# Seven block products in place of eight in the channel half of an MLP-mixer, with the token products of all batches ahead of it

## The chip, the core and the metric

The kernel runs on one core of one Trainium2 chip. The metric is device time in microseconds (us): the median of three runs was 979.88 us (979.80 to 980.96). Five engines work side by side, each on its own queue in order: TensorE (PE, with its weight loads shown as PEld), VectorE (DVE), ScalarE (ACT), GpSimd (POOL) and SyncE (SP, which issues the transfers). Semaphores order them. TensorE writes to PSUM; VectorE and ScalarE take results out of it.

## What is computed

A clustered attention, and behind it one mixer layer. Sizes: 4 batches, 8 heads of 64, sequence 768, model width 512, token width 256, channel width 1536. All is float32 (the weights arrive as float64).

```python
attn_out = _attn_ref(**attn_kwargs)          # masked softmax attention, (B, H, S, D)
x = attn_out.transpose(0, 2, 1, 3).reshape(B, S, H * D)
xt = x.transpose(0, 2, 1)
h = np.maximum(xt @ w_tok1, 0.0) @ w_tok2    # token products
u = x + h.transpose(0, 2, 1)
h2 = np.maximum(u @ w_ch1, 0.0) @ w_ch2      # channel products
return (u + h2)
```

## The kernel before

**Attention** fills the first 373 us: 16 pairs of heads, six steps each, written as one loop over `m` in which scores, exponentials, sums and values of neighbouring steps alternate. While it runs, the float64 weights of the token products and of the first channel product are turned into float32 pieces: ScalarE makes two parts (L184, L186), VectorE three operations (L191, L196, L201), GpSimd one addition (L208). The attention result of batch b lies in `xs[b]`, six blocks of 128 tokens by 512.

**Token products** of a batch: `tok1` (L439), two groups of six 128x512 matmuls with a relu behind each (L427 on VectorE, L429 on ScalarE in turn), then `tok2` (L448), six groups of two, each followed by an addition into `xs[b]` on VectorE (L451). Those of batch 0 come right behind the attention, those of batch b+1 among the channel products of batch b.

**Channel products** go by half batches of 384 tokens: `turn_u` transposes u on TensorE (L460, twelve 128x128) and ScalarE copies it out (L463); `ch1` (L470) makes twelve groups of four 128x384 matmuls, relu behind each; `ch2` (L479) three groups of twelve 128x512 matmuls, an addition on VectorE (L484) and a transfer out (L485). A float32 matmul stands in the profile as two MATMUL records, called passes here, each with a weight load of its own.

**Order.** Nothing reorders the work: each engine's queue holds the instructions in the order in which the program's lines make them (the lists `ends` and `weights` say what is made beside what). The weights of `ch2` are converted during the first `ch1` groups. Behind batch 0, `fits` (L493 to L507) checks with a few VectorE operations and one tiny matmul (L504) that the fast path was valid, and every engine loads three counts into a register (L512), which decides at the program's end whether the general path runs.

Of the kernel before, what the change touches and what calls it, by code (L numbers as in the profile page):

```python
# [18 lines left out]
P = 128  # L19
NJ = S // P  # L20
# [26 lines left out]
def kernel(  # L47
# [46 lines left out]
    h1pool = pool("h1pool", 1)  # L94
# [15 lines left out]
    ohs = [const.tile([P, 2, NJ, P], BF16, name=f"oh{i}") for i in range(2)]  # L110
# [3 lines left out]
    wt1 = const.tile([P, NJ, DTOK], F32, name="wt1")  # L114
    wt2 = const.tile([P, NT, NJ, P], F32, name="wt2")
    wc1 = const.tile([P, NF, DCH], F32, name="wc1")
# [25 lines left out]
    def weight_pieces(names):  # L142

        if "tok" in names:
            src = moe_w_tok1.rearrange("(p j) t -> p (j t)", p=P)
            dst = wt1.rearrange("p j t -> p (j t)")
            for c in range(0, NJ * DTOK, WMAX):
                yield dst[:, c : c + WMAX], src[:, c : c + WMAX]
            for t in range(NT):
                for p0 in range(0, P, P // 2):  # L150
                    yield (
                        wt2[:, t, :, p0 : p0 + P // 2].rearrange("t j p -> t p j"),
                        moe_w_tok2[t * P : (t + 1) * P, p0 * NJ : (p0 + P // 2) * NJ],
                    )
        if "ch1" in names:
            for c in range(0, DCH, WMAX):
                for f in range(NF):
                    yield wc1[:, f, c : c + WMAX], moe_w_ch1[f * P : (f + 1) * P, c : c + WMAX]
        if "ch2" in names:
            for ct in range(NCT):  # L160
                yield pools["wc2"][:, ct], moe_w_ch2[ct * P : (ct + 1) * P]

    def weight_steps(pool, names):
# [46 lines left out]
        pieces = list(weight_pieces(names))  # L210
# [211 lines left out]
    turns = [0]  # L422
# [13 lines left out]
    def tok1(b, t):  # L436
        pf = mtile([P, DM], "ph1")
        for j in range(NJ):
            nc.tensor.matmul(  # L439
                pf, lhsT=wt1[:, j, t * P : (t + 1) * P], rhs=xs[b][:, j],  # L440
                start=(j == 0), stop=(j == NJ - 1),
            )
        relu(h1[:, t], pf)

    def tok2(b, j):
        pu = mtile([P, DM], "pu")
        for t in range(NT):
            nc.tensor.matmul(  # L448
                pu, lhsT=wt2[:, t, j], rhs=h1[:, t], start=(t == 0), stop=(t == NT - 1)
            )  # L450
        nc.vector.tensor_tensor(out=xs[b][:, j], in0=pu, in1=xs[b][:, j], op=ALU.add)  # L451

    uTs = {}

    def turn_u(b, hf):
        uT = uTs[b, hf] = pools["mlp"].tile([P, NF, HJ, P], F32, name="uT", bufs=2)
# [19 lines left out]
    def ch2(b, hf, i):
        po = mtile([P, DM], "po2")
        for ct in range(NCT):
            nc.tensor.matmul(  # L479
                po, lhsT=pools["h2"][:, ct, i * P : (i + 1) * P], rhs=pools["wc2"][:, ct],  # L480
# [102 lines left out]
    for item in ends:  # L583
        item()
# [235 lines left out]
```

## Time and profile before

| | us |
|---|---|
| median of three runs | 979.88 |
| the profiled execution's own time | 979.91 |
| its span (first to last instruction) | 978.1 |
| PE busy | 953.1 (97%) |
| DVE busy | 364.5 (37%) |
| ACT busy | 263.2 (27%) |
| POOL busy | 48.8 (5%) |

Durations of instructions are from the one profiled execution. A busy time is the union of an engine's instructions; matmuls overlap each other, so the mean of one pass is longer than the distance from pass to pass. In the chain of waits the row "PE pc L470 x96" with 30.96 us means 96 passes one behind the other.

### The profile page before, as it was taken

To read this page: it belongs to the slowest core of one execution; us is meant where nothing else is said; L and a number is where in the kernel's file an instruction comes from. 1 tells how busy PE (TensorE), PEld (TensorE's weight loads), DVE (VectorE), ACT (ScalarE), POOL (GpSimd) and SP (SyncE) were. 2 spreads that over 40 slices of the span, in tenths; PEclk is the share of its full clock that TensorE was granted. 3 is DMA by queue.
4 is the path that set the end of the run, shared out by engine and by line. 5 is a ranking of instruction groups with operands and counts; after the bars stand their busy time and mean duration, and the time that the engine had idled before them with its cause. 6 is when DMAs were issued, how large, how long until landed. Compare 5 with 4: busy or idle time off the path is not lost.

```text
span 978.1 us, 10328 instructions
## 1 busy us (share of the span) xinstructions
PE 953.1 (97%) x4227; PEld 461.8 (47%) x4227; DVE 364.5 (37%) x554; ACT 263.2 (27%) x421; POOL 48.8 (5%) x40
## 2 busy tenths in 40 slices
PE   4999999999999999999999899999999999999997
PEld 2444444444444444554544454554554554554553
DVE  4778777787878652660102100101100101100100
ACT  3655566566565552430000010000110000110000
POOL 1001101010111000230000000000000000000000
PEclk9999999999999999999999999999999999999999
DMA  9253433333342001320000000000000000000000
GB/s 194 66 102 78 86 92 71 92 70 93 72 111 46 1 23 43 108 87 25 8 0 22 11 1 21 11 0 11 21 1 21 11 1 11 22 0 22 11 8 29
DMA packets 112823, 41.68 MB, mean 43 GB/s; under 512 B 101632, under 2 KB 105728, under 8 KB 112768
## 3 DMA queue, kind: packets, MB, share of 16 engines
q1 hardware_dynamic: 109632, 40.55, 16.8%
q10 hardware_dynamic: 3136, 0.39, 0.3%
q8 instruction: 35, 0.57, 0.3%
q14 instruction: 20, 0.16, 0.1%
HBM read 34.64 MB, written 6.29 MB: 42 GB/s over the span
## 4 chain that ended last, share of the span: by engine, by line
PE 97%; DVE 1%; ACT 1%; DMA 0%; issue 0%; ACTq 0%; DVEq 0%; SPq 0%
PE po L479 25%; PE pc L470 25%; PE sc L340 17%; PE av L369 14%; PE pu L448 4%; PE ph L439 4%; PE px L404 2%; PE po L316 1%; PE pr L278 1%; PE den L385 1%; PE pt L460 1%; DMA raw<-in_moe_w_ch_dram 0%; ACTq L133 0%; DVE qkT L267 0%; DVE x L484 0%
## 5 line engine op out<-in xcount | busy, mean ns | idle before, releaser
L470 PE MATMUL pc<-uT,wc 128*128 128x384 f32 x768 | 251.4, 489 | 1.6 <-issue 1.6
L479 PE MATMUL po<-wc,h 128*128 128x512 f32 x576 | 249.5, 592 | 0.0
L470 PEld LDWEIGHTS pc<-uT,wc 128*128 128x128 f32 x768 | 146.3, 191 | 104.0 <-issue 6.1
L346 ACT ACTIVATE ex<-sc 128x768 f32<-128x768 f32 x192 | 145.3, 808 | 117.3 <-PE sc L340 117.3
L479 PEld LDWEIGHTS po<-wc,h 128*128 128x128 f32 x576 | 109.2, 190 | 135.3 <-issue 133.7
L369 PE MATMUL av<-ex,va 128*64 128x384 f32 x768 | 145.1, 499 | 0.0
L359 DVE TENSOR_TENSOR sum<-sum,ex 128x768 f32<-128x768 f32 x128 | 133.5, 1043 | 30.6 <-ACT ex L346 22.2
L340 PE MATMUL sc<-qkT 64*128 64x384 f32 x768 | 140.7, 486 | 0.0
L429 ACT ACTIVATE h<-pc 128x384 f32<-128x384 f32 x48 | 23.6, 492 | 359.2 <-PE pc L470 359.2
L484 DVE TENSOR_TENSOR x<-po,x 128x512 f32<-128x512 f32 x24 | 16.6, 691 | 261.5 <-PE po L479 261.5
L427 DVE TENSOR_SCALAR h<-pc 128x384 f32<-128x384 f32 x48 | 26.8, 557 | 189.2 <-PE pc L470 189.2
L369 PEld LDWEIGHTS av<-ex,va 128*64 128x64 f32 x768 | 46.6, 136 | 86.5 <-issue 82.7
L340 PEld LDWEIGHTS sc<-qkT 64*128 64x128 f32 x768 | 71.2, 188 | 31.8 <-issue 0.6
L340 PE MATMUL sc<-ohT 64*128 64x384 bf16 x384 | 48.5, 329 | 1.8 <-ACT ohT L318 1.0
L208 POOL TENSOR_TENSOR wc<-wT,wup 128x512 int32<-128x512 int32 x24 | 35.5, 1480 | 259.8 <-DVE wT L201 143.3
L448 PE MATMUL pu<-h,wt 128*128 128x512 f32 x96 | 42.1, 593 | 0.0
L463 ACT COPY uT<-pt 128x384 f32<-128x384 f32 x32 | 13.0, 491 | 107.9 <-PE pt L460 107.9
L439 PE MATMUL ph<-x,wt 128*128 128x512 f32 x96 | 42.0, 593 | 0.0
L410 DVE TENSOR_TENSOR x<-px,rcps 128x384 f32<-128x384 f32 x32 | 17.8, 557 | 49.5 <-PE px L404 47.9
L355 DVE TENSOR_TENSOR sum<-ex 128x768 f32<-128x768 f32 x32 | 30.2, 944 | 6.3 <-ACT ex L346 5.7
L267 DVE STREAM_TRANSPOSE qkT<-qk 128x768 f32<-128x768 f32 x32 | 29.3, 953 | 0.0
L439 PEld LDWEIGHTS ph<-x,wt 128*128 128x128 f32 x96 | 18.2, 190 | 22.4 <-issue 21.6
(63 smaller groups left out, 376.1 us busy)
## 6 DMA issues: line engine op xcount, KB each, us to landing
raw<-in_moe_w_ch_dram SPq DMA_DIRECT2D x24, 512.0 KB, 3.8
qk<-in_k_dram SPq DMA_DIRECT2D x64, 96.0 KB, 4.0
va<-in_v_dram SPq DMA_DIRECT2D x16, 384.0 KB, 3.4
out_dram<-x SPq DMA_DIRECT2D x24, 256.0 KB, 2.0
qk<-in_q_dram SPq DMA_DIRECT2D x60, 96.0 KB, 3.0
raw<-in_moe_w_tok_dram SPq DMA_DIRECT2D x3, 512.0 KB, 5.3
raw<-in_moe_w_tok_dram SPq DMA_DIRECT2D x4, 384.0 KB, 3.6
qk<-in_q_dram ACTq DMA_DIRECT2D x4, 96.0 KB, 3.5
```

Source lines behind the costliest of these rows:

```text
L208: nc.gpsimd.tensor_tensor(out=dst.bitcast(I32), in0=T, in1=up, op=ALU.add)
L267: nc.vector.transpose(out=st["T"][:, a].rearrange("p j t -> p (j t)"), in_=st["qk"][:, a].rearrange("p j i d -> p (j i d)"),)
L340: nc.tensor.matmul(scs[i][:, h, 0:HS], lhsT=src[rows, 1, j0 + i], rhs=src[rows, 0, js], start=start, stop=not start,)
L346: nc.scalar.activation(out=ex, in_=scs[i][:, :, 0:HS], func=ACT.Exp, scale=SM_SCALE)
L355: nc.vector.tensor_tensor(out=acc, in0=e[0], in1=e[1], op=ALU.add)
L359: nc.vector.tensor_tensor(out=acc, in0=acc, in1=e[i], op=ALU.add)
L369: nc.tensor.matmul(st["av"][h * D : (h + 1) * D], lhsT=st["va"][:, h, j], rhs=ex[:, h], start=(j == 0), stop=(j == NJ - 1),)
L427: nc.vector.tensor_scalar_max(out=dst, in0=src, scalar1=0.0)
L439: nc.tensor.matmul(pf, lhsT=wt1[:, j, t * P : (t + 1) * P], rhs=xs[b][:, j], start=(j == 0), stop=(j == NJ - 1),)
L448: nc.tensor.matmul(pu, lhsT=wt2[:, t, j], rhs=h1[:, t], start=(t == 0), stop=(t == NT - 1))
L470: nc.tensor.matmul(pc, lhsT=wc1[:, f, ct * P : (ct + 1) * P], rhs=uTs[b, hf][:, f], start=(f == 0), stop=(f == NF - 1),)
L479: nc.tensor.matmul(po, lhsT=pools["h2"][:, ct, i * P : (i + 1) * P], rhs=pools["wc2"][:, ct], start=(ct == 0), stop=(ct == NCT - 1),)
```

## The change: seven products by Winograd's scheme

A product of two matrices cut into 2x2 blocks takes eight block products. Winograd's form of Strassen's scheme takes seven: it first makes four sums of blocks on each side (S1 to S4 from the left factor, T1 to T4 from the right), and combines the seven products into the four result blocks c11, c12, c21, c22. The change writes both channel products so.

For `ch1` the left factor is the weight `wc1` (blocks of 256 of the model width by 768 channels), the right one the transposed u of a whole batch (256 of the width by 384 tokens). A chunk is 128 channels of each half: seven products of two 128x384 matmuls. For `ch2` the left factor is the hidden layer, whose sums `hS` are made on VectorE as its blocks come out, the right one `wc2`; a chunk is 128 tokens of each half: seven products of three 128x256 matmuls. The hidden layer is handled in two parts, so each batch has 6 chunks of `ch1` and 6 of `ch2`. Three PSUM tiles serve a chunk: X takes four products one after the other on top of each other, and between them its state is copied out (`p1`, `u2`) or added (`c22`); Z takes two, Y one. The last product of a chunk (`end`) is issued behind the first product of the next chunk.

The sums of the weights are made once, by VectorE, in pieces called `left_weights` (w1s, from `wc1`) and `right_weights` (w2s, from `wc2`); the sums of u once per batch in `turn_u`. The token products of all four batches now come right behind the attention, and beside them the conversion of `wc2` and the weights' sums. `fits` moves to the end of the token products.

```diff
-    h1pool = pool("h1pool", 1)
+    wc1pool = pool("wc1pool", 1)
+    tokens = fast.enter_context(ExitStack())
+    tokpool = pool("tokpool", 1, tokens)
...
     def mtile(shape, name):
-        return pools["ps_m"].tile(shape, F32, tag="m", name=name)
-    h1 = h1pool.tile([P, NT, DM], F32, name="h1")
+        turns[1] += 1
+        return pools["ps_m"].tile(shape, F32, tag="XZ"[turns[1] % 2], name=name)
+    h1s = {}
...
+    def left_weights():
+        w = W["ch1"]
+        half = DCH // 2
+        A = {
+            f"A{i + 1}{j + 1}": w[:, 2 * j : 2 * j + 2, half * i : half * i + half]
+            for i in range(2)
+            for j in range(2)
+        }
+        extra = pools["wsums"].tile([P, 3, 2, half], F32, name="w1s")
+        A["S1"], A["S2"], A["S4"] = (extra[:, i] for i in range(3))
+        yield lambda: add(A["S1"], A["A21"], A["A22"])
+        yield lambda: sub(A["S2"], A["S1"], A["A11"])
+        yield lambda: sub(A["A21"], A["A11"], A["A21"])
+        yield lambda: sub(A["S4"], A["A12"], A["S2"])
+        A["S3"] = A["A21"]
+        pools["A"] = A
...
+        yield lambda: sub(B_["T1"], B_["B12"], B_["B11"])
+        yield lambda: sub(B_["T2"], B_["B22"], B_["T1"])
+        yield lambda: sub(B_["B12"], B_["B12"], B_["B22"])
+        yield lambda: sub(B_["T4"], B_["B21"], B_["T2"])
+        B_["T3"] = B_["B12"]
...
+    def turn_u(b, n):
+        if n == 0:
+            pools["uT"] = pools["mlp"].tile([P, 2, NF, HS], F32, name="uT")
+            pools["uTs"] = pools["mlp"].tile([P, 3, NF // 2, HS], F32, name="uTs")
+        uT, uTs = pools["uT"], pools["uTs"]
         for f in range(NF):
             pt = ps_w.tile([P, HJ, P], F32, tag="w", name="pt")
             for i in range(HJ):
                 nc.tensor.transpose(
-                    out=pt[:, i], in_=xs[b][:, HJ * hf + i, f * P : (f + 1) * P], identity=ident
-                )
-            nc.scalar.copy(out=uT[:, f], in_=pt)
...
+                    out=pt[:, i], in_=xs[b][:, HJ * n + i, f * P : (f + 1) * P], identity=ident
+                )
+            nc.scalar.copy(out=uT[:, n, f], in_=pt.rearrange("p i t -> p (i t)"))
+        if n == 1:
+            R = {"B11": uT[:, 0, 0:2], "B21": uT[:, 0, 2:4], "B22": uT[:, 1, 2:4]}
+            R["T1"], R["T2"], R["T4"] = (uTs[:, i] for i in range(3))
+            R["T3"] = b12 = uT[:, 1, 0:2]
+            sub(R["T1"], b12, R["B11"])
+            sub(R["T2"], R["B22"], R["T1"])
+            sub(R["T3"], R["B22"], b12)
+            sub(R["T4"], R["B21"], R["T2"])
+            pools["R"] = R
...
+    late = []
+    def chunk(n, product, done):
+        def ptile(tag):
+            if tag == "Y":
+                return ps_w.tile([P, n], F32, tag="w", name="pY")
+            return pools["ps_m"].tile([P, n], F32, tag=tag, name="p" + tag)
+        X = ptile("X")
+        product(X, "A11", "B11", True)
+        if late:
+            late.pop()()
+        done("p1", X)
+        Z = ptile("Z")
+        product(Z, "S1", "T1", True)
+        done("p5", Z)
+        Y = ptile("Y")
+        product(Y, "A12", "B21", True)
+        done("c11", Y)
+        product(X, "S2", "T2", False)
+        done("u2", X)
+        product(Z, "S4", "B22", False)
+        done("c12", Z)
+        product(X, "S3", "T3", False)
+        done("c22", X)
+        def end():
+            product(X, "A22", "T4", False)
+            done("c21", X)
+        late.append(end)
+    def ch1_chunk(part, i):
+        c = 3 * part + i
+        if i == 0:
+            pools["h2"] = {
+                k: pools["mlp"].tile([P, 3, HS], F32, name="h" + k)
+                for k in ("A11", "A12", "A22", "S1", "S2", "S3", "S4")
+            }
+        A, R, h2 = pools["A"], pools["R"], pools["h2"]
+        kept = {}
+        def product(psum, a, r, start):
+            for k in range(2):
+                nc.tensor.matmul(
+                    psum, lhsT=A[a][:, k, c * P : (c + 1) * P], rhs=R[r][:, k],
+                    start=start and k == 0, stop=k == 1, skip_group_check=not start,
+                )
+        def done(name, psum):
+            if name in ("p1", "p5", "u2"):
+                kept[name] = pools["mlp"].tile([P, HS], F32, name=name, bufs=2)
+                nc.scalar.copy(out=kept[name], in_=psum)
+            elif name == "c11":
+                a = h2["A11"][:, i]
+                add(a, psum, kept["p1"])
+                nc.scalar.activation(out=a, in_=a, func=ACT.Relu)
+            elif name == "c12":
+                kept["c12"] = pools["mlp"].tile([P, HS], F32, name="c12", bufs=2)
+                add(kept["c12"], psum, kept["u2"])
+            elif name == "c22":
+                a = h2["A22"][:, i]
+                add(a, psum, kept["p5"])
+                nc.scalar.activation(out=a, in_=a, func=ACT.Relu)
+                nc.vector.scalar_tensor_tensor(
+                    out=h2["S3"][:, i], in0=kept["c12"], scalar=0.0, in1=h2["A11"][:, i],
+                    op0=ALU.max, op1=ALU.subtract,
+                )
+                nc.vector.scalar_tensor_tensor(
+                    out=h2["S1"][:, i], in0=kept["c12"], scalar=0.0, in1=a,
+                    op0=ALU.max, op1=ALU.add,
+                )
+                sub(h2["S2"][:, i], h2["S1"][:, i], h2["A11"][:, i])
+            else:
+                a = h2["A12"][:, i]
+                nc.scalar.activation(out=a, in_=psum, func=ACT.Relu)
+                sub(h2["S4"][:, i], a, h2["S2"][:, i])
+        chunk(HS, product, done)
+    def ch2_chunk(b, part, i):
+        h2, Bw = pools["h2"], pools["B"]
+        u = {
+            f"c{r + 1}{c + 1}": xs[b][:, HJ * r + i, 256 * c : 256 * c + 256]
+            for r in range(2)
+            for c in range(2)
+        }
+        kept = {}
+        takes = {"p1": "c11", "p5": "c22", "u2": "c12"}
+        gives = {"c11": "p1", "c22": "p5", "c12": "u2"}
+        def product(psum, a, w, start):
+            for k in range(3):
+                nc.tensor.matmul(
+                    psum, lhsT=h2[a][:, k, i * P : (i + 1) * P], rhs=Bw[w][:, 3 * part + k],
+                    start=start and k == 0, stop=k == 2, skip_group_check=not start,
+                )
+        def done(name, psum):
+            if name in takes:
+                kept[name] = pools["mlp"].tile([P, DM // 2], F32, name=name, bufs=2)
+                add(kept[name], psum, u[takes[name]])
+            else:
+                add(u[name], psum, kept[gives[name]] if name in gives else u[name])
+                if part == 1 and name in ("c12", "c21"):
+                    j = i + HJ * (name == "c21")
+                    nc.sync.dma_start(
+                        out[b].rearrange("(p j) m -> p j m", p=P)[:, j], xs[b][:, j]
+                    )
+        chunk(DM // 2, product, done)
...
-    ends = [lambda t=t: tok1(0, t) for t in range(NT)] + [lambda j=j: tok2(0, j) for j in range(NJ)]
+    ends = [lambda t=t: tok1(0, t) for t in range(NT)]
+    for b in range(B):
+        if b + 1 < B:
+            ends += [lambda b=b, t=t: tok1(b + 1, t) for t in range(NT)]
+        ends += [lambda b=b, j=j: tok2(b, j) for j in range(NJ)]
...
-                pools["ps_m"] = pool("ps_m", 4, space=PSUM)
+                pools["ps_m"] = pool("ps_m", 2, space=PSUM)
...
-    for item in ends:
-        item()
     attention.close()
-    pools["wc2"] = ctx.enter_context(
-        tc.tile_pool(name="wc2p", bufs=1, side="right", reuse_waits="tile")
-    ).tile([P, NCT, DM], F32, name="wc2")
+    other = fast.enter_context(ExitStack())
+    W["ch2"] = pool("wc2pool", 1, other, side="right").tile([P, NCT, DM], F32, name="wc2")
+    pools["wsums"] = pool("wsums", 1, other, side="right")
+    staging = ExitStack()
+    beside = list(left_weights())
+    beside[4:4] = weight_steps(pool("mstage", 2, staging), W, ("ch2",))
+    beside += right_weights()
+    while ends:
+        for _ in range(-(-len(beside) // len(ends))):
+            beside.pop(0)()
+        ends.pop(0)()
+    both = fits()
+    staging.close()
+    tokens.close()
     pools["mlp"] = pool("mlp", 1)
-    mstage = pool("mstage", 2)
-    weights = list(weight_steps(mstage, ("ch2",)))
-    for _ in range(3):
-        weights.pop(0)()
-    turn_u(0, 0)
+    for n in range(2):
+        turn_u(0, n)
     for b in range(B):
-        for hf in range(2):
-            for ct in range(NCT):
-                ch1(b, hf, ct)
-                if weights:
-                    weights.pop(0)()
-                if hf == 0 and ct == 2:
-                    turn_u(b, 1)
-            nxt = b + 1 < B and hf == 1
-            if nxt:
-                for t in range(NT):
-                    tok1(b + 1, t)
-            for i in range(HJ):
-                ch2(b, hf, i)
-                if nxt and i == 0:
-                    for j in range(NJ):
-                        tok2(b + 1, j)
-                if nxt and i == 1:
-                    turn_u(b + 1, 0)
-        if b == 0:
-            both = fits()
+        for part in range(2):
+            for i in range(3):
+                ch1_chunk(part, i)
+            for i in range(3):
+                ch2_chunk(b, part, i)
+                if part == 1 and i < 2 and b + 1 < B:
+                    turn_u(b + 1, i)
+    late.pop()()```

VectorE's queue at the end of the token products. Before, behind the additions of batch 0 (`pu`) come the conversions of `wc2`, between the relus of `ch1`:

```order
L451 TENSOR_TENSOR x_105<-pu,x_105 128x512 x2
L191 TENSOR_SCALAR wh<-wh 128x512
L196 TENSOR_SCALAR wh<-wh 128x512
L201 SCALAR_TENSOR_TENSOR wT<-raw,wh 128x512
L427 TENSOR_SCALAR h_3548<-pc_3549 128x384
```

Now the last batch's additions (x_111) have the last conversions and the four sums of `wc2` (w2s, and one in place) between them, and `fits` right behind:

```order
L200 TENSOR_SCALAR wh<-wh 128x512
L205 TENSOR_SCALAR wh<-wh 128x512
L210 SCALAR_TENSOR_TENSOR wT<-raw,wh 128x512
L463 TENSOR_TENSOR x_111<-pu,x_111 128x512
L474 TENSOR_TENSOR w2s<-wc_3521 128x1536
L463 TENSOR_TENSOR x_111<-pu,x_111 128x512
L474 TENSOR_TENSOR w2s<-wc_3521,w2s 128x1536
L463 TENSOR_TENSOR x_111<-pu,x_111 128x512
L474 TENSOR_TENSOR wc_3521<-wc_3521 128x6x256
L463 TENSOR_TENSOR x_111<-pu,x_111 128x512
L474 TENSOR_TENSOR w2s<-wc_3521,w2s 128x1536
L463 TENSOR_TENSOR x_111<-pu,x_111 128x512
```

The conversions of `wc2` moved from under the `ch1` groups to under the token products of the last batches, and the sums are new.

TensorE's queue around `fits`. Before, it stands between the last `ch2` group of batch 0 and the `ch1` of batch 1:

```order
L479 MATMUL po_3964<-wc_3501,h_3800 128x512 x12
L504 MATMUL pn<-good,ones 1x3
L512 TENSOR_LOAD count x3
L470 MATMUL pc_4035<-uT,wc_104 128x384 x4
L470 MATMUL pc_4041<-uT,wc_104 128x384 x4
```

Now it stands between the last token products and the transposes of batch 0:

```order
L460 MATMUL pu<-h_3531,wt_106 128x512 x12
L460 MATMUL pu<-h_3616,wt_106 128x512 x12
L671 MATMUL pn<-good,ones 1x3
L679 TENSOR_LOAD count x3
L523 MATMUL pt<-ident,x_108 128x128 x24
L584 MATMUL pX<-uT,wc_107 128x384 x2
```

`fits` thus has VectorE's token additions and weight sums ahead of it, and the whole mixer behind it.

TensorE's queue where `ch1` meets `ch2`. Before, groups of four 128x384 and then of twelve 128x512:

```order
L470 MATMUL pc_3738<-uT,wc_104 128x384 x4
L470 MATMUL pc_3749<-uT,wc_104 128x384 x4
L479 MATMUL po_3755<-wc_3501,h_3548 128x512 x12
L479 MATMUL po_3770<-wc_3501,h_3548 128x512 x12
L479 MATMUL po_3785<-wc_3501,h_3548 128x512 x12
```

Now products of two 128x384, the late product of `ch1` behind the first of `ch2`, then products of three 128x256:

```order
L584 MATMUL pZ<-uTs,w1s 128x384 x2
L584 MATMUL pY<-uT,wc_107 128x384 x2
L584 MATMUL pX<-uTs,w1s 128x384 x2
L584 MATMUL pZ<-uT,w1s 128x384 x2
L584 MATMUL pX<-uT,wc_107 128x384 x2
L635 MATMUL pX<-wc_3521,hA_3882 128x256 x3
L584 MATMUL pX<-uTs,wc_107 128x384 x2
L635 MATMUL pZ<-w2s,hS_3885 128x256 x3
L635 MATMUL pY<-wc_3521,hA_3883 128x256 x3
L635 MATMUL pX<-w2s,hS_3886 128x256 x3
L635 MATMUL pZ<-wc_3521,hS_3888 128x256 x3
```

The moving operand of `ch2` went from 512 columns to 256, and X is written again two products after it was written last.

## Rows read from the trace of the kernel before

**Rows 1.** The page, busy time of each engine, share of the span and instructions

```profile
PE 953.1 (97%) x4227; PEld 461.8 (47%) x4227; DVE 364.5 (37%) x554; ACT 263.2 (27%) x421; POOL 48.8 (5%) x40
```

**Rows 2.** The page, chain that ended last, by line

```profile
PE po L479 25%; PE pc L470 25%; PE sc L340 17%; PE av L369 14%; PE pu L448 4%; PE ph L439 4%; PE px L404 2%; PE po L316 1%; PE pr L278 1%; PE den L385 1%; PE pt L460 1%; DMA raw<-in_moe_w_ch_dram 0%; ACTq L133 0%; DVE qkT L267 0%; DVE x L484 0%
```

**Rows 3.** The chain in order of time, from 380 us: start us, us, what

```profile
396.37 1.44 PE pt L460 x12
...
431.89 30.90 PE po L479 x72
462.79 30.96 PE pc L470 x96
493.75 10.30 PE ph L439 x24
```

**Rows 4.** Instruction groups by form, weight loads: busy us, mean ns | idle before

```profile
L479 PEld LDWEIGHTS po<-wc,h 128*128 128x128 f32 x576 | 109.2, 190 | 135.3 <-issue 133.7 <-POOL wc L208 0.2
L369 PEld LDWEIGHTS av<-ex,va 128*64 128x64 f32 x768 | 46.6, 136 | 86.5 <-issue 82.7 <-ACT wup L186 3.8
```

**Rows 5.** Timeline from 397 us: start us, us, engine, what [idle before]

```profile
397.64 7.91 PE L470 MATMUL pc<-uT,wc 128*128 128x384 f32 x24
...
400.43 0.56 DVE L427 TENSOR_SCALAR h<-pc 128x384 f32<-128x384 f32 x1 [1.81 <-PE pc L470]
...
408.12 0.55 PE L460 MATMUL pt<-ident,x 128*128 128x128 f32 x3 [1.59 <-ACT uT L463]
```

**Rows 6.** Instruction groups by form, VectorE and ScalarE

```profile
L355 DVE TENSOR_TENSOR sum<-ex 128x768 f32<-128x768 f32 x32 | 30.2, 944 | 6.3 <-ACT ex L346 5.7
...
L451 DVE TENSOR_TENSOR x<-pu,x 128x512 f32<-128x512 f32 x24 | 16.6, 691 | 31.2 <-PE pu L448 31.2
...
L463 ACT COPY uT<-pt 128x384 f32<-128x384 f32 x32 | 13.0, 491 | 107.9 <-PE pt L460 107.9
```

**Rows 7.** Timeline from 397 us, one conversion step of `wc2`

```profile
397.01 0.42 DVE L191 TENSOR_SCALAR wh<-wh 128x512 f32<-128x512 f32 x1
...
397.46 0.43 DVE L196 TENSOR_SCALAR wh<-wh 128x512 uint32<-128x512 uint32 x1
...
397.92 0.69 DVE L201 SCALAR_TENSOR_TENSOR wT<-raw,wh 128x512 uint32<-128x512 uint32 x1
...
398.83 1.27 POOL L208 TENSOR_TENSOR wc<-wT,wup 128x512 int32<-128x512 int32 x1 [80.80 <-DVE wT L201]
```

**Rows 8.** Timeline from 402 us, VectorE beside GpSimd

```profile
402.65 1.32 POOL L208 TENSOR_TENSOR wc<-wT,wup 128x512 int32<-128x512 int32 x1 [2.55 <-DVE wT L201]
402.88 1.38 DVE L196 TENSOR_SCALAR wh<-wh 128x512 uint32<-128x512 uint32 x1
...
405.18 1.27 POOL L208 TENSOR_TENSOR wc<-wT,wup 128x512 int32<-128x512 int32 x1 [1.21 <-DVE wT L201]
...
405.59 0.56 DVE L427 TENSOR_SCALAR h<-pc 128x384 f32<-128x384 f32 x1 [0.55 <-PE pc L470]
```

**Rows 9.** The page, transfers of weights: KB each, median us to landing

```profile
raw<-in_moe_w_ch_dram SPq DMA_DIRECT2D x24, 512.0 KB, 3.8
```

**Rows 10.** The chain in order of time, around the check behind batch 0

```profile
546.74 0.69 DVE x L484
547.43 0.18 DVE inside L493
...
548.97 0.20 PE pn L504 x2
...
549.42 1.33 issue
550.75 9.67 PE pc L470 x24
```

**Rows 11.** A stretch behind the check: busy us of PE, PEld, DVE, ACT, POOL, granted clock

```profile
553.80:555.20 1.40, 1.40 (x4) 0.78 (x3) 0.01 (x1) 0.00 (x0) 0.00 (x0) 0.50 0.00 0
```

**Rows 12.** The chain's last piece

```profile
972.31 0.69 DVE x L484
```

More of the change, by code (lines that the diff above doesn't have):

```diff
@@ L109 @@
     cnd = const.tile([P, NF, 2, C], F32, name="cnd")
-    ohs = [const.tile([P, 2, NJ, P], BF16, name=f"oh{i}") for i in range(2)]
+    ohs = [small.tile([P, 2, NJ, P], BF16, name=f"oh{i}", bufs=1) for i in range(2)]
     rcps = const.tile([P, 2 * NPAIR, 2, HJ], F32, name="rcps")
     cells = const.tile([P, NPAIR], F32, name="cells")
-    wt1 = const.tile([P, NJ, DTOK], F32, name="wt1")
-    wt2 = const.tile([P, NT, NJ, P], F32, name="wt2")
-    wc1 = const.tile([P, NF, DCH], F32, name="wc1")
+    W = {
+        "tok1": tokpool.tile([P, NJ, DTOK], F32, name="wt1"),
+        "tok2": tokpool.tile([P, NT, NJ, P], F32, name="wt2"),
+        "ch1": wc1pool.tile([P, NF, DCH], F32, name="wc1"),
+    }
     state = {}
@@ L419, in half_out @@
             state.pop(g)
-    turns = [0]
+    turns = [0, 0]
     def relu(dst, src):
@@ L448, in tok2, with sub, add, right_weights @@
             nc.tensor.matmul(
-                pu, lhsT=wt2[:, t, j], rhs=h1[:, t], start=(t == 0), stop=(t == NT - 1)
+                pu, lhsT=W["tok2"][:, t, j], rhs=h1s[b][:, t], start=(t == 0), stop=(t == NT - 1)
             )
         nc.vector.tensor_tensor(out=xs[b][:, j], in0=pu, in1=xs[b][:, j], op=ALU.add)
-    uTs = {}
-    def turn_u(b, hf):
-        uT = uTs[b, hf] = pools["mlp"].tile([P, NF, HJ, P], F32, name="uT", bufs=2)
+    def sub(dst, a, b):
+        nc.vector.tensor_tensor(out=dst, in0=a, in1=b, op=ALU.subtract)
+    def add(dst, a, b):
+        nc.vector.tensor_tensor(out=dst, in0=a, in1=b, op=ALU.add)
+    def left_weights():
[14 more added lines that the diff above has]
+        pools["A"] = A
+    def right_weights():
+        w = W["ch2"]
+        B_ = {
+            f"B{i + 1}{j + 1}": w[:, 6 * i : 6 * i + 6, 256 * j : 256 * j + 256]
+            for i in range(2)
+            for j in range(2)
+        }
+        extra = pools["wsums"].tile([P, 3, NCT // 2, DM // 2], F32, name="w2s")
+        B_["T1"], B_["T2"], B_["T4"] = (extra[:, i] for i in range(3))
+        yield lambda: sub(B_["T1"], B_["B12"], B_["B11"])
[3 more added lines that the diff above has]
+        B_["T3"] = B_["B12"]
+        pools["B"] = B_
+    def turn_u(b, n):
[3 more added lines that the diff above has]
+        uT, uTs = pools["uT"], pools["uTs"]
         for f in range(NF):
@@ L476, in ch2 @@
[L476 to L480, printed above, removed]
-                start=(ct == 0), stop=(ct == NCT - 1),
-            )
-        u = xs[b][:, HJ * hf + i]
-        nc.vector.tensor_tensor(out=u, in0=po, in1=u, op=ALU.add)
-        nc.sync.dma_start(out[b].rearrange("(p j) m -> p j m", p=P)[:, HJ * hf + i], u)
+            nc.scalar.copy(out=uT[:, n, f], in_=pt.rearrange("p i t -> p (i t)"))
@@ L633, in gtile @@
             return gps.tile(shape, dt, tag="g", name=name)
+        GW = {
+            "tok1": gone.tile([P, NJ, DTOK], F32, name="gwt1"),
+            "tok2": gone.tile([P, NT, NJ, P], F32, name="gwt2"),
+            "ch1": gone.tile([P, NF, DCH], F32, name="gwc1"),
+            "ch2": gone.tile([P, NCT, DM], F32, name="gwc2"),
+        }
+        with tc.tile_pool(name="gstage", bufs=1) as gstage:
+            for step in weight_steps(gstage, GW, list(GW)):
+                step()
         msc = gone.tile([P, 2], F32, name="msc")
@@ L755, in general @@
                     nc.tensor.matmul(
-                        pu, lhsT=wt2[:, t, j], rhs=h1[:, t], start=(t == 0), stop=(t == NT - 1)
+                        pu, lhsT=GW["tok2"][:, t, j], rhs=h1[:, t], start=(t == 0), stop=(t == NT - 1)
                     )
```

78 lines of the change are left out of this document (39 added, 39 removed).

## The prediction

> **What bounds the kernel now.** I read the page's busy times first: TensorE is busy for 953.1 of 978.1 us, the next engine for 364.5 [rows 1]. The chain that ended last says the same in another way: nearly all of it is TensorE, half of it the two channel products, 25% each [rows 2]. So time is worth what TensorE's passes take, plus the few stretches in which it stands still. Read in order of time, the chain gives the rate of an undisturbed stream: 96 passes of 384 columns in 30.96 us, 0.3225 us each, 72 of 512 in 30.90, 0.4292 each; token products go at the second rate (24 in 10.30), transposes at 0.120 (12 in 1.44) [rows 3]. A pass takes less than its record's mean since passes overlap.
>
> **Fewer passes.** ch1 had 768 passes of 384 columns and gets 4 x 6 x 7 x 2 x 2 = 672: 96 fewer, x 0.3225 = -31.0 us. ch2 had 576 passes of 512, x 0.4292 = 247.2 us, and gets 4 x 6 x 7 x 3 x 2 = 1008 of 256. No row shows that width. The two rates lie on a line through nearly nothing (0.0008 us a column, 0.002 left over), so 256 columns give 2 x 0.3225 - 0.4292 = 0.2158 us, and 217.6 in all: -29.6 us. The line holds as long as the weight load stays hidden. A load of 128 columns takes 0.190 us, one of 64 columns 0.136 [rows 4], so the 64 further columns cost 0.054 and the part that grows with width is 0.107 for 128. A load of 0.190 still fits under 0.2158, by 0.026. Bounds: 0.2158 if hidden, 0.2158 + 0.107 = 0.323 if not at all; below the line nothing is expected, since the streaming alone gives it. I take 0.2158, as both measured widths show no trace of the load.
>
> The Trainium skill speaks against this: "TensorE: Matmul & The Clock Gate", Part 3, The mechanism, says that a weight load overlaps matmuls in flight only where it goes to another row group. All passes here use all rows, so by that rule each would cost load plus stream. The rates of the trace contradict it at 384 and 512 columns, and no row shows 256; it is the third rival below.
>
> **The waits inside a chunk.** A ch1 chunk is 28 passes, 9.03 us, a ch2 chunk 42, 9.06. X is read out between two of its products, with one other product of 1.29 us in between (4 x 0.3225 or 6 x 0.2158). The stretch from TensorE's last pass to the reader is seen at 400.43: the eight passes from 397.64 end at 400.22, so 0.21 us [rows 5]. ScalarE's copy of 384 takes 0.49. For VectorE the rows give 0.944 at 768 and 0.691 at 512 [rows 6], 0.001 us a column: 0.44 at 256, while the row at 400.43 shows 0.56 at 384. So X is free again 0.70 us (ScalarE) or 0.77 (VectorE) after its product, under a cover of 1.29. The other waits are longer away. Per ch1 chunk VectorE has seven operations, 3.9 us, and ScalarE six, 2.9, under 9.03. Behind turn_u VectorE has four sums of 768 columns, 3.8 us, ahead of the copy-out of X. TensorE needs that 5.2 us after the transposes (four products), VectorE is there at about 4.9: covered, barely. I cost all this at nothing; if the cover fails by 0.3 us at one wait of each of 48 chunks, it is +14 us. Bounds 0 and 48 x 0.77 = 37.
>
> **Stalls that go.** TensorE waited 1.59 us for the copies of the second transposes behind the conversions on ScalarE [rows 5]; those conversions are no longer there: -1.6. The check behind batch 0 goes from there: its gap is counted below.
>
> **The token stage.** Now VectorE and not TensorE sets the pace at its end. From the start of the last twelve tok2 groups TensorE has 12 x 4 x 0.4292 = 20.6 us. VectorE has twelve additions of 0.69 [rows 6], seven conversions and four sums of 1536 columns. A conversion is 0.42 + 0.43 + 0.69 = 1.54 us on VectorE, and 0.2 us later 1.3 on GpSimd [rows 7]. Beside GpSimd a VectorE operation from SBUF to SBUF stood until GpSimd had ended: 1.38 us in place of 0.43; one that reads PSUM ran its usual 0.56 [rows 8]. So in each period an addition (0.69, from PSUM) runs beside GpSimd, and the next conversion waits for GpSimd's end at 1.5 us: 1.5 + 1.5 = 3.0 us a period, where TensorE needs 1.72. A sum of 1536 is 0.944 + 768 x 0.001 = 1.70 us. In sequence: first addition done at 1.72 + 0.21 + 0.69 = 2.6; first conversion 4.1; six more at 3.0, 22.1; GpSimd's last addition ends at 23.6; four pairs of sum and addition, 2.39 each, 33.2. The transfers (3.8 us to landing, three buffers) [rows 9] follow at one per 3.0 us and don't add.
>
> Behind it stands the check, from 547.43 to 550.75: 3.3 us until TensorE goes on, with 1.33 of it the counts' way into the registers [rows 10]. All of it comes after VectorE's last addition: 36.5 us, TensorE's own 20.6 taken off: +15.9. What goes is the old place's gap: VectorE took up TensorE's last group at 546.74, 0.2 us after its passes, so TensorE stood for 550.75 - 546.53 = 4.2 us: -4.2. Bounds: were GpSimd no hindrance, a period would be 2.23 and the term +10.6; did the additions wait for it too, 3.7 and +21. For the additions the nearest row is the unhindered one, and I take it.
>
> The Trainium skill, "SBUF — State Buffer", Who interferes with whom, has the rule behind it: the shared ports hold up a VectorE operation in a two-port mode or with two SBUF inputs, and not one with a single SBUF input. The additions have one, so by the rule too +15.9; their form beside GpSimd is in no row.
>
> **The clock.** Behind the old gap the granted clock fell to 0.50 [rows 11], half of 2.4 GHz: the 24 passes took 9.67 us in place of 7.74, 1.9 us more [rows 10]. The new gap is longer, some 10 us between the last token product and the transposes. I put the same 1.9 for it, bounds 0 and 3.9 (twice), and take the old one off: 0 together.
>
> **Ends.** The 24 transposes of batch 0 wait for ScalarE's copies: +0.3. At the very end the late product waits 0.7 us for VectorE with nothing to cover it, and the last addition is 256 wide, 0.44 in place of 0.69 [rows 12]: +0.4. The attention is untouched.
>
> **Sum.** -31.0 - 29.6 - 1.6 - 4.2 - 1.9 + 15.9 + 1.9 + 0.3 + 0.4 = -49.8. The profiled execution took 979.91 us (span 978.1, 1.8 around it), as good as the median of 979.88. So 979.9 - 49.8 = 930.1 us.
>
> **Rivals.**
> - *The waits in the chunks show.* X serves four products, with one product as cover each time. Against it: 0.77 of 1.29 us used, and both helpers busy for less than half. For it: both are strictly in order, and a semaphore wait ahead of nearly every product is something the old streams did not have. With 0.3 us a chunk: 944 us; with 0.77, 967.
> - *The token stage is hidden after all*, since VectorE may run ahead of TensorE in the first groups of the stage: at the lower bound 10.6, and with a clock that stays up, 923 us.
> - *The weight loads set the pace of the 256 columns.* From 0.265 us a pass on (49.8 / 1008 = 0.049 above the line) the change is slower than before; with 0.323 it is 930.1 + 108 = 1038 us. For it: 0.026 us is all that is left over, and 0.190 need not be all that a load takes up. Against it: at 0.120 us a transpose of 128 columns, with its load, streams faster than 0.190, so loads themselves overlap [rows 3, 4]. This is the skill's rule as a mechanism of this kernel; the two widths of the trace leave it a small chance. In between, at 0.23, 945 us.
>
> **How the numbers follow.** My forecast 0.68, with a range of its own from 924 to 938 (the token stage's and the clock's bounds); the waits 0.16; the hidden token stage 0.09; weight loads 0.07, of which 0.04 on the slower side. The range reaches from 921 to 946 and so takes in the milder half of the first and third rivals. About 0.2% is what a measurement of this kernel can tell from no change; only the weight loads bring it there or beyond: faster 0.95, same 0.01, slower 0.04.
>
> **What would show it.** In the changed profile: ch1 chunks of 28 passes in 9.03 us, ch2 chunks of 42 in 9.06, one behind the other; VectorE's busy share near 9 tenths ahead of the mixer, a TensorE gap of about 10 us there, ended by the check; additions unhindered beside GpSimd. It would be wrong if TensorE showed a recurring wait for ScalarE or VectorE at X, or weight loads without idle time between them in ch2 and passes well over 0.216.

## The result, and the profile after

The changed kernel takes 929.96 us (median of 4 runs, 929.0 to 930.29), the kernel before 980.42 beside it: a ratio of 0.9485, with an interval of 0.9471 to 0.9499. The forecast was 930.1. The profiled execution has a span of 928.0 us, 50.1 less than before; the sum said 49.8.

The page's busy times, one row for all engines (busy time, share of the span, number of instructions), to be held against [rows 1]:

```profile
PE 894.4 (96%) x4563; PEld 527.2 (57%) x4563; DVE 508.6 (55%) x842; ACT 310.6 (33%) x517; POOL 48.5 (5%) x40
```

TensorE has 336 instructions more and 58.7 us less work, VectorE 144 us more work, which delays TensorE at one place only, ahead of the mixer, and for a moment at the very end. First the mixer: a window of it (its ends and length, then busy time and count of TensorE, weight loads, VectorE, ScalarE, GpSimd, then the granted clock and what the transfers took), and two neighbouring chunks of either kind in the chain of waits (start, us, instructions).

```profile
478.56:918.92 440.36, 440.36 (x1741) 324.39 (x1741) 171.91 (x349) 79.80 (x169) 0.00 (x0) 1.00 0.04 14
```

```profile
485.01 3.87 PE pX L584 x12
494.04 3.87 PE pX L584 x12
...
512.13 3.88 PE pX L635 x18
521.19 3.88 PE pX L635 x18
```

TensorE stands still for nothing in 440 us. The steps between neighbours are 494.04 - 485.01 = 9.03 us for 28 passes of 384 columns and 521.19 - 512.13 = 9.06 for 42 of 256, as forecast; three products of six passes, one behind the other, take 3.88, so a pass of 256 columns takes 0.2156 us.

Now what TensorE does wait for from 400 us on (operation and line that waits, what it waits for, us in total, times, longest):

```profile
PE pn L671 <- DVE good L669: 9.3, 1, 9.3
PE pu L460 <- DVE x L463: 2.9, 3, 1.0
PE pt L523 <- issue: 1.6, 1, 1.6
PE pX L635 <- DVE x L477: 0.5, 1, 0.5
```

The first three are the end of the token stage, the last is the late product at the very end. The steady part of the token stage on the timeline, VectorE and GpSimd (start, us, operation):

```profile
444.72 0.68 DVE L463 TENSOR_TENSOR x<-pu,x 128x512 f32<-128x512 f32 x1
444.95 1.28 POOL L217 TENSOR_TENSOR wc<-wT,wup 128x512 int32<-128x512 int32 x1 [1.67 <-DVE wT L210]
445.32 1.19 DVE L200 TENSOR_SCALAR wh<-wh 128x512 f32<-128x512 f32 x1
446.54 0.43 DVE L205 TENSOR_SCALAR wh<-wh 128x512 uint32<-128x512 uint32 x1
447.06 0.69 DVE L210 SCALAR_TENSOR_TENSOR wT<-raw,wh 128x512 uint32<-128x512 uint32 x1
447.67 0.68 DVE L463 TENSOR_TENSOR x<-pu,x 128x512 f32<-128x512 f32 x1
```

A period is 447.67 - 444.72 = 2.95 us. GpSimd's addition starts while VectorE adds from PSUM, and that addition keeps its 0.68; the conversion's first operation, from SBUF to SBUF, is drawn out from 0.42 to 1.19, to GpSimd's end at 444.95 + 1.28 = 446.23 and a little beyond. That is what [rows 8] had let expect. The Trainium skill ("SBUF — State Buffer", Who interferes with whom) has as its rule for the shared ports that an operation with at most one SBUF input, outside the two-port modes, is not held up; the additions' 0.68 beside GpSimd bears it out. The prediction called this form unseen, but the trace of before does hold it, in the attention: a VectorE operation with one input from PSUM and one from SBUF, beside GpSimd, at its usual 0.56.

```profile
316.76 1.27 POOL L208 TENSOR_TENSOR wc<-wT,wup 128x512 int32<-128x512 int32 x1 [14.11 <-DVE wT L201]
...
317.24 0.56 DVE L410 TENSOR_TENSOR x<-px,rcps 128x384 f32<-128x384 f32 x1
```

The end of the token stage, on VectorE, GpSimd and TensorE:

```profile
459.44 0.68 DVE L463 TENSOR_TENSOR x<-pu,x 128x512 f32<-128x512 f32 x1
459.67 1.26 POOL L217 TENSOR_TENSOR wc<-wT,wup 128x512 int32<-128x512 int32 x1 [1.67 <-DVE wT L210]
460.04 2.51 DVE L474 TENSOR_TENSOR w2s<-wc 128x1536 f32<-128x1536 f32 x1
...
460.18 1.98 PE L460 MATMUL pu<-h,wt 128*128 128x512 f32 x4 [0.95 <-DVE x L463]
...
463.07 1.74 DVE L474 TENSOR_TENSOR w2s<-wc,w2s 128x1536 f32<-128x1536 f32 x1
...
469.27 0.68 DVE L463 TENSOR_TENSOR x<-pu,x 128x512 f32<-128x512 f32 x1
...
471.17 0.17 DVE L669 TENSOR_REDUCE good<-inside 128x1 f32<-128x16 f32 x1
471.49 0.19 PE L671 MATMUL pn<-good,ones 128*1 128x3 f32 x2 [9.33 <-DVE good L669]
473.28 5.28 PE L523 MATMUL pt<-ident,x 128*128 128x128 f32 x24 [1.60 <-issue]
```

VectorE's last token addition ends at 469.95, and 3.3 us later, behind the check and the counts' way into the registers, TensorE goes on. From its last token product to the transposes TensorE has stood for 9.3 + 1.6 us, with the check's two passes between them: a gap of 11.1 us, ended by the check. The first weight sum takes 2.51 and not the 1.74 of the next: it too stood beside a GpSimd addition. The transposes take 5.28 us; the windows around them tell why (the number behind GpSimd's is the granted clock):

```profile
470.00:473.28 3.28, 0.19 (x3) 0.15 (x3) 1.45 (x8) 0.00 (x0) 0.00 (x0) 0.50 0.00 0
473.30:475.60 2.30, 2.30 (x11) 2.30 (x12) 0.00 (x0) 1.09 (x3) 0.00 (x0) 0.50 0.00 0
475.60:478.30 2.70, 2.70 (x15) 2.70 (x14) 0.40 (x1) 2.05 (x5) 0.00 (x0) 0.50 0.00 0
```

All 24 run at the lower level, 1.2 GHz, as the passes behind the old gap did [rows 11].

### The profile page after: what moved, and what is told of

Same layout as the page of the kernel before. It is cut to its first block, busy times and chain, and to the rows that moved or that the text cites. A ratio compares the mean times of both kernels' runs of the same rounds, so it can differ in the third digit from the quotient of the medians.

```text
span 928.0 us, 11533 instructions
## 1 busy us (share of the span) xinstructions
PE 894.4 (96%) x4563; PEld 527.2 (57%) x4563; DVE 508.6 (55%) x842; ACT 310.6 (33%) x517; POOL 48.5 (5%) x40
## 4 chain that ended last, share of the span: by engine, by line
PE 94%; DVE 4%; ACT 0%; issue 0%; ACTq 0%; DVEq 0%
PE sc L349 18%; PE av L378 15%; PE pX L635 13%; PE pX L584 13%; PE pZ L635 7%; PE pZ L584 7%; PE ph L451 4%; PE pY L635 3%; PE pY L584 3%; PE pu L460 2%; PE px L413 2%; PE po L325 2%; PE pt L523 2%; PE pr L287 1%; PE den L394 1%; DVE wh L200 1%
## 5 line engine op out<-in xcount | busy, mean ns | idle before, releaser
L355 ACT ACTIVATE ex<-sc 128x768 f32<-128x768 f32 x192 | 145.3, 809 | 117.6 <-PE sc L349 117.6
L378 PEld LDWEIGHTS av<-ex,va 128*64 128x64 f32 x768 | 46.6, 136 | 86.5 <-issue 82.7
L584 PE MATMUL pX<-uT,wc 128*128 128x384 f32 x192 | 67.2, 486 | 0.0
L592 ACT COPY p<-pX 128x384 f32<-128x384 f32 x24 | 11.4, 475 | 132.3 <-PE pX L584 132.3
L349 PE MATMUL sc<-ohT 64*128 64x384 bf16 x384 | 48.8, 331 | 1.6 <-ACT ohT L327 1.0
L217 POOL TENSOR_TENSOR wc<-wT,wup 128x512 int32<-128x512 int32 x24 | 35.2, 1468 | 287.0 <-DVE wT L210 178.5
L584 PEld LDWEIGHTS pX<-uT,wc 128*128 128x128 f32 x192 | 36.5, 190 | 23.7
L460 PE MATMUL pu<-h,wt 128*128 128x512 f32 x96 | 42.5, 596 | 2.9 <-DVE x L463 2.9
L451 PE MATMUL ph<-x,wt 128*128 128x512 f32 x96 | 42.1, 594 | 0.0
L477 DVE TENSOR_TENSOR c<-pZ,u 128x384 f32<-128x384 f32 x24 | 13.4, 557 | 48.9 <-PE pZ L584 48.9
L477 DVE TENSOR_TENSOR x<-pX,x 128x256 f32<-128x256 f32 x24 | 10.2, 423 | 49.3 <-PE pX L635 49.3
L477 DVE TENSOR_TENSOR hA<-pY,p 128x384 f32<-128x384 f32 x24 | 13.4, 557 | 41.0 <-PE pY L584 41.0
L635 PE MATMUL pX<-w2s,hA 128*128 128x256 f32 x144 | 35.1, 380 | 0.5 <-DVE x L477 0.5
L635 PE MATMUL pX<-wc,hA 128*128 128x256 f32 x144 | 35.0, 379 | 0.0
L635 PE MATMUL pZ<-w2s,hS 128*128 128x256 f32 x144 | 35.0, 379 | 0.0
L635 PE MATMUL pY<-wc,hA 128*128 128x256 f32 x144 | 35.0, 379 | 0.0
## 6 DMA issues: line engine op xcount, KB each, us to landing
raw<-in_moe_w_ch_dram SPq DMA_DIRECT2D x24, 512.0 KB, 3.8
raw<-in_moe_w_tok_dram SPq DMA_DIRECT2D x3, 512.0 KB, 5.2
```

The source lines that it names most:

```text
L217: nc.gpsimd.tensor_tensor(out=dst.bitcast(I32), in0=T, in1=up, op=ALU.add)
L349: nc.tensor.matmul(scs[i][:, h, 0:HS], lhsT=src[rows, 1, j0 + i], rhs=src[rows, 0, js], start=start, stop=not start,)
L355: nc.scalar.activation(out=ex, in_=scs[i][:, :, 0:HS], func=ACT.Exp, scale=SM_SCALE)
L378: nc.tensor.matmul(st["av"][h * D : (h + 1) * D], lhsT=st["va"][:, h, j], rhs=ex[:, h], start=(j == 0), stop=(j == NJ - 1),)
L451: nc.tensor.matmul(pf, lhsT=W["tok1"][:, j, t * P : (t + 1) * P], rhs=xs[b][:, j], start=(j == 0), stop=(j == NJ - 1),)
L460: nc.tensor.matmul(pu, lhsT=W["tok2"][:, t, j], rhs=h1s[b][:, t], start=(t == 0), stop=(t == NT - 1))
```

## The experiments

Seven kernels, each with one edit to three, all measured against the kernel before. The first three try the changed kernel's parts, the last four its one long stall.

**Eight products.** The order of the changed kernel (token products of all batches first, chunks of the same blocks), but eight block products and no block sums. Two blocks of the hidden layer (c12 and c21) change places in it; the number and the shapes of its products stay those of eight.

```
-        product(X, "A11", "B11", True)
-        ... (seven products, with their sums and the late one)
+        for tag, name, terms in (
+            ("X", "c11", (("A11", "B11"), ("A12", "B21"))),
+            ("Z", "c12", (("A11", "B12"), ("A12", "B22"))),
+            ("Y", "c21", (("A21", "B11"), ("A22", "B21"))),
+            ("X", "c22", (("A21", "B12"), ("A22", "B22"))),
+        ):
+            t = ptile(tag)
+            product(t, *terms[0], True)
+            product(t, *terms[1], False)
+            done(name, t)
```

> Eight block products of the same shapes in place of seven, no sums of weights, u or hidden layer; token products first and the check behind them, as in the changed kernel. My theory (the seventh-eighth of the passes is the whole gain of the mixer, at 0.3225 and 0.2158 us a pass; the sums lie beside it and cost TensorE nothing): ch1 96 passes more, +31.0; ch2 144 passes more, +31.1; VectorE spared the four sums of wc2 ahead of the check, 2.5 + 3 x 1.74 = -7.7. 930 + 62.1 - 7.7 = 984 us. Rival (the seven-product form loses some of its gain again to waits at X and to sums, and the shorter time comes in part from the moved token products and check): less than 984 by what is lost there, 970 if 14 us are.

Measured 984.07 us, ratio 1.0035 (1.0021 to 1.0048). Its stall on the timeline of TensorE:

```profile
464.31 0.19 PE L609 MATMUL pn<-good,ones 128*1 128x3 f32 x2 [2.27 <-DVE good L607]
466.10 5.32 PE L510 MATMUL pt<-ident,x 128*128 128x128 f32 x24 [1.60 <-issue]
```

That is the 984 expected, and not the rival's 970. So the new order by itself gains nothing, it loses 3 us (the narrower passes, 1152 x 0.2156 - 247.2 = 1.2, among them); seven products for eight are worth 984.07 - 929.96 = 54.1. That splits into the passes, 96 x 0.3225 + 144 x 0.2156 = 62.0, less 473.28 - 466.10 = 7.2 us by which the sums of the weights on VectorE make the stall longer; 0.7 is left for the ends.

**No late product.** The last product of a chunk is issued at once and not behind the next chunk's first, so nothing covers the read of X.

```
-        late.append(end)
+        end()
```

> The last product of a chunk right behind the one before it, not behind the next chunk's first product: X's read-out by VectorE loses its cover in all 48 chunks. My theory (the read-out takes 0.21 + 0.56 + 0.05 us in ch1, 0.21 + 0.42 + 0.06 in ch2, and the product in between covers all of it): 24 x 0.82 + 23 x 0.69 = +35.5 us, 965 us; PE waits for VectorE 47 times at X. Rival (the cover holds only in part and the changed kernel already pays there): a smaller rise, below 950.

Measured 970.86 us, 40.9 more. The waits, and one of each kind on the timeline:

```profile
PE pX L584 <- DVE hA L477: 15.8, 24, 0.7
PE pX L635 <- DVE x L477: 12.4, 24, 0.5
```

```profile
505.63 0.56 DVE L477 TENSOR_TENSOR hA<-pX,p 128x384 f32<-128x384 f32 x1 [0.66 <-PE pX L584]
...
506.33 1.53 PE L584 MATMUL pX<-uTs,wc 128*128 128x384 f32 x4 [0.74 <-DVE hA L477]
...
507.70 0.59 PE L635 MATMUL pX<-wc,hA 128*128 128x256 f32 x2
```

The product ahead starts at 504.14 and, streaming, would be followed at 505.43: TensorE goes on 0.90 us late, more than the idle time of 0.74, since the records of four passes reach over 1.45 us while products follow one another every 1.29. And the four passes behind the wait take 507.70 - 506.33 = 1.37 in place of 1.29. In the ch2 chunks it is 0.69 and 0.10. 24 x 0.98 + 23 x 0.79 = 41.7 comes within 0.8 of the 40.9 measured; my 35.5 had each late start right within 0.1 us (0.82 and 0.69 against 0.90 and 0.69) and no cost for starting again. The waits are there, and in the changed kernel, where no X wait but the last shows, the product in between hides all of them: this is what the first rival's price would have been.

**Passes of 128 columns.** ch2's 1008 passes of 256 columns as 2016 of 128, with twice the weight loads and the same columns.

```
-            for k in range(3):
-                nc.tensor.matmul(psum, lhsT=h2[a][...], rhs=Bw[w][:, 3 * part + k], ...)
+            for half in range(2):
+                cols = slice(128 * half, 128 * half + 128)
+                for k in range(3):
+                    nc.tensor.matmul(psum[:, cols], lhsT=h2[a][...],
+                                     rhs=Bw[w][:, 3 * part + k, cols], ...)
```

> Each 256-column matmul of ch2 as two of 128 columns: 2016 passes, the same columns, twice the weight loads. It asks how near the 256-column pass is to the point where loads set the pace. If loads stay hidden at 128 too: 0.109 us a pass, 220 us, +2.6, 933 us. If a load's record of 0.190 us is the floor: 383 us, +165, 1095 us. If a load costs what the transposes show (0.120, of which 0.053 columns) with twice the load's width part: about 0.174, 351 us, +133, 1063 us. If load and columns add up (0.107 + 0.109): 435 us, +218, 1148 us.

Measured 936.61 us, 6.65 more. From the chain of waits three products on X, one behind the other, from the groups by shape one tile's weight loads (count, busy us, mean ns, idle before them):

```profile
511.55 4.02 PE pX L637 x36
```

```profile
L637 PEld LDWEIGHTS pY<-wc,hA 128*128 128x128 f32 x288 | 34.1, 192 | 0.0
```

36 passes in 4.02 us are 0.1117 each, where the line through 384 and 512 columns gives 0.109. Each has its own load, whose record is 0.192 us long: loads follow one another at 0.112 us, without idle time, and still hardly hold up the stream. At 256 columns a load has 0.2156 and, by this pace, needs about half. The margin of 0.026 that I gave it was a record's length taken for a rate; the row on transposes, which I set against it, was the better witness [rows 3, 4]. By the rule of the Trainium skill ("TensorE: Matmul & The Clock Gate", Part 3, The mechanism), under which a load overlaps matmuls in flight only where its row group differs, this kernel would have been slower than before by far; the run contradicts it. The same section also lets a load for a background weight buffer go ahead, which the prediction left out and which this run neither shows nor excludes.

**The check taken early.** VectorE's part of the check stands ahead of the last part of the token stage, the matmul and the rounding four groups in (two of `tok1`, two of `tok2`), and the loads of the counts at the very end.

```
+    good = fits()
     while ends:
+        if len(ends) == 18:
+            count = count_up(good)
...
-    both = fits()
...
     late.pop()()
+    both = fetch(count)
```

> The check's VectorE operations at the start of the second half of the token stage, its tiny matmul some products later, the loads of the three counts at the program's very end; all else as in the changed kernel. My theory (behind the token products TensorE waits for VectorE, which has the conversions and sums ahead of the check; without the check the transposes and the first product run beside that work, and TensorE's next wait is for the sums of u, which VectorE starts at 469.95): the second product of the mixer starts near 470.9 in place of 479.7, -8.8 us; the clock may fall in a gap of some 4 us, up to +1.9: 921 to 923 us. Rival (the check's own 3.3 us is all that is lost there): 926.7 us. Rival (the loads of the counts cost as much at the end): 925 us or more.

Measured 924.97 us, ratio 0.9432 (0.9417 to 0.9448). The timeline of TensorE, and VectorE's sum that it waits for:

```profile
462.28 3.14 PE L523 MATMUL pt<-ident,x 128*128 128x128 f32 x24
...
470.15 0.94 DVE L474 TENSOR_TENSOR uTs<-uT 128x768 f32<-128x768 f32 x1
471.15 2.66 PE L584 MATMUL pZ<-uTs,w1s 128*128 128x384 f32 x4 [3.78 <-DVE uTs L474]
```

The transposes now run straight behind the token products at full clock, 3.14 us: the half clock cost 5.28 - 3.14 = 2.1 in the changed kernel. What is late next is VectorE, whose first sum of batch 0 stands behind its four additions and sums. pZ starts at 471.15, 8.5 us earlier than the 479.69 of the changed kernel, as expected, but then takes 2.66 in place of 1.45: the clock fell after this gap too, and the product after next starts 475.53 - 471.15 = 4.4 us behind pZ in place of 2.6, so 1.8 of the 8.5 are lost again. And the end is longer: from VectorE's last instruction to the end of the span 7.0 us in place of 5.2. With both losses the time lies 2 us above the 921 to 923 expected, at the second rival's 925.

**The same, with the counts loaded in mid mixer.**

```
                 ch1_chunk(part, i)
+                if b == 1 and part == 0 and i == 1:
+                    both = fetch(count)
...
-    both = fetch(count)
```

> The kernel with the check taken early (924.97 us), with the three loads of the counts moved from the very end to the second batch of the mixer. Theory (the 1.7 us by which its end was longer were the loads, which in the middle of a stream cost only what TensorE's queue does not work off meanwhile): 923.3 us, with nothing longer behind the last addition than in the changed kernel. Rival (every engine that loads a count stands still for it, TensorE too, 1.3 us wherever it is): 924.6 to 925.

Measured 923.18 us (0.9401 to 0.9429). Its last VectorE instruction:

```profile
915.59 0.42 DVE L477 TENSOR_TENSOR x<-pX,x 128x256 f32<-128x256 f32 x1 [1.65 <-PE pX L635]
```

It stands where it stood in the run before (915.60), and the span ends 5.5 us behind it, at 921.5. So the loads are free here within a stream and cost 1.5 us at the end, as they and the rounding cost 1.6 ahead of the transposes; the rival's 924.6 to 925 is refuted. Why 5.5 is still 0.3 more than the changed kernel's 5.2 stays open.

**The conversions first.** Only the order of the work beside the token products: three conversions (with their parts on ScalarE and GpSimd) beside one token item, early, the sums after them; the check in its place.

```
-    beside = list(left_weights())
-    beside[4:4] = weight_steps(pool("mstage", 2, staging), W, ("ch2",))
-    beside += right_weights()
+    plan = [conv[0:3], conv[3:6], lw[0:1], [], lw[1:2], [], lw[2:3], [], conv[6:9], conv[9:12]]
+    plan += [conv[12:13], [], conv[13:14], [], lw[3:4], [], rw[0:1], [], rw[1:2], [], rw[2:3], rw[3:4]]
```

> The order of VectorE's own work in the token stage is changed and nothing else: the conversions of the second channel weights go first, three beside one token item, so that they lie beside the first twelve tok1 groups, and the eight sums come after them; the check keeps its place behind the stage. Theory (TensorE's gap behind the token products is what VectorE is late there: 6 to 7 steps of 2.95 us against TensorE's 1.72 in the last twelve groups, and then the check): with no conversion left beside the additions, VectorE ends 8 to 9 us earlier, the check with its 3.3 us stays: a gap of 6 to 7 us in place of 15.0, 921.5 us; the clock still falls for the transposes. Rival 1 (the slower pace only moves, because conversions packed three to an item hold up the additions and so tok2's buffers): TensorE waits 5 us or more in the first half of the stage, 926 or more. Rival 2 (VectorE's lag is not what decides, the check alone is): 930, no change.

Measured 923.21 us (0.94 to 0.9429). TensorE's waits from 400 us on:

```profile
PE pn L671 <- DVE good L669: 4.3, 1, 4.3
PE pt L523 <- issue: 1.6, 1, 1.6
PE pu L460 <- DVE x L463: 0.9, 1, 0.9
...
PE pu L460 <- ACT h L438: 0.3, 1, 0.3
```

```profile
466.43 5.35 PE L523 MATMUL pt<-ident,x 128*128 128x128 f32 x24 [1.59 <-issue]
```

The wait at the check fell from 9.3 to 4.3, those on the additions from 2.9 to 0.9. My 921.5 was 1.7 too low: the last twelve groups start at 437.92, and the stage still loses 466.43 - 437.92 - 20.6 = 7.9 us in place of 15.0, where I had 6 to 7. Of that, 1.2 are waits in the earlier groups, of the kind that this run's first rival named. The second rival, no change, is refuted. The clock fell as before (5.35 us for the transposes), with a gap of 6.1 us ahead of them as with one of 11.1.

**All three.** The conversions first, the check early with its counts in mid mixer, and the four sums of the second channel weights behind p5 of the first four chunks.

```
+        if aside:
+            aside.pop(0)()
...
+    aside += rw
```

> The conversions first, the check taken up early with its counts loaded in the second batch of the mixer, and the four sums of the second channel weights issued behind p5 of the first four chunks, where VectorE is free more than half of the time. Theory: nothing is left behind the token products but VectorE's last addition and ScalarE's copies: a gap of 1 us in place of 15.0 and no fall of the clock (2.1): 930.0 - 14 - 2.1 = 914, with 913 to 916 for the counts' loads. Rival 1 (the waits in the chunks have little cover, so four sums of 1.7 us among them stall TensorE): 4 x 1.5 = 6 us given back, 920. Rival 2 (the clock falls whatever the gap): 916 to 917.

Measured 915.08 us (914.67 to 915.5), ratio 0.9332 (0.9319 to 0.9344): within the expected 913 to 916, and neither rival. TensorE from 400 us on, its waits, and the transposes:

```profile
PE pu L460 <- DVE x L463: 0.6, 1, 0.6
PE pX L638 <- DVE x L477: 0.5, 1, 0.5
PE pu L460 <- ACT h L438: 0.5, 1, 0.5
PE pX L587 <- issue: 0.3, 1, 0.3
```

```profile
460.43 3.14 PE L523 MATMUL pt<-ident,x 128*128 128x128 f32 x24
```

The transposes start 473.28 - 460.43 = 12.85 us earlier and end 2.1 sooner after that; the sums among the chunks cost about 0.5. The granted clock is 1.00 from 396 to 905 us. This version beats the changed kernel by 1.6%, and TensorE is busy for 98% of its span.

## Why the prediction was right, step by step

- *Fewer passes*: -60.6 forecast. The chunks take 9.03 and 9.06 us, the same numbers. The run with eight products shows that the whole gain is here: with the new order and without the seven products there is none. The line through 384 and 512 columns held at 256, and at 128 within 3% (0.1117 against 0.109). Right, though the margin of the load was wrong, and with it the 0.07 that I gave the third rival was too much.
- *The waits in the chunks*: nothing, as costed. That this is cover and not absence, the run without the late product shows: 40.9 us without it, where my upper bound was 37. The bound was too low, for it left out the start again of 0.08 to 0.10 us behind each wait.
- *The token stage*: +15.9 forecast, 473.28 - 437.68 - 20.6 = 15.0 measured (437.68 is where the stream puts the start of the last twelve groups). The period was 2.95 in place of 3.0, a pair of sum and addition 2.27 (467.00 to 469.27) in place of 2.39, the check 3.3; TensorE's gap was 11.1 us where about 10 was said. The mechanism is shown: with conversions out of the way the gap shrinks, with the check and the four sums out of the way too it is gone (the sums were not moved by themselves). The second rival's lower bound, GpSimd no hindrance, was wrong from the first period on; that the stage can be hidden takes another order, that of the last run.
- *The clock*: +1.9 forecast, 2.1 measured, by the run whose transposes go at full clock in 3.14 us. The +0.3 for the start of the transposes is in those 3.14: 24 at 0.120 would be 2.88, so 0.26.
- *The end*: +0.4 forecast; 0.52 us of wait for the late product, less 0.27 for the narrower last addition, about +0.3, as the timeline of the changed kernel shows:

```profile
920.26 0.42 DVE L477 TENSOR_TENSOR x<-pX,p 128x256 f32<-128x256 f32 x1 [0.87 <-PE pX L635]
920.74 1.16 PEld L635 LDWEIGHTS pX<-w2s,hA 128*128 128x128 f32 x6 [0.92 <-DVE x L477]
920.74 1.56 PE L635 MATMUL pX<-w2s,hA 128*128 128x256 f32 x6 [0.52 <-DVE x L477]
922.34 0.42 DVE L477 TENSOR_TENSOR x<-pX,x 128x256 f32<-128x256 f32 x1 [1.66 <-PE pX L635]
```

- *The attention* was called untouched, but in the profiled execution the first token product starts 0.3 us later than before (373.34 against 373.07); over the nine profiled executions that start lies between 373.07 and 373.58.
- *The stalls that go*, -1.6, -4.2 and -1.9, were not tried apart. With the other terms as measured (passes 31.0 + 247.2 - 1008 x 0.2156 = 60.9) the sum leaves them 50.1 + 15.0 + 2.1 + 0.3 + 0.3 + 0.3 - 60.9 = 7.2, where 7.7 was forecast; how the missing 0.5 us is spread stays open.

The mechanism was right in every stretch that a run tried. That 930.1 met 929.96 so closely is luck all the same: the token stage cost 0.9 us less than forecast and the passes saved 0.3 more, while the stalls gave back 0.5 less, and the clock and the attention cost 0.5 more.

## What to carry to other kernels

Where one engine is busy for 97% of the time, a saving in its passes is the saving of the kernel, but only as far as the helper engines' new work finds cover: count the work that moves to them in the stretch where it must be done, not over the span. Read the rate of a stream from the distance of starts, not from the length of records, for loads above all. A wait cost its length and a start again here (0.08 to 0.10 us each, 47 times), so a product in between that hides the wait whole saves both, and a shorter wait only the first.

## What the runs showed of the hardware that was not expected

Weight loads of 128 columns follow one another every 0.112 us though each record is 0.192 long, and passes of 128 columns with a load each still take 0.1117. Behind a wait of 0.5 to 0.7 us TensorE's next four or six passes take 0.08 to 0.10 us longer, at a granted clock of 1.00. The granted clock stayed at 1.00 through 47 such waits (in the run without the late product), and fell behind one wait of 3.78 us: a window behind it, in the run with the check taken early, has 0.61.

```profile
471.15:475.50 4.35, 4.35 (x8) 2.36 (x9) 2.70 (x3) 0.48 (x1) 0.00 (x0) 0.61 0.00 0
```
